# Spreading the output projection of a decode attention kernel over its rolled loop

## The chip, the cores and the metric

One core of one Trainium2 chip. The metric is device time in microseconds (us), the median of the fast runs; lower is better. The profile's "span" is some 1.8 us shorter than the time.

## The reference, cut to what matters

One decode step: 32 query heads share 8 groups of keys and values (4 heads to a group), 65536 keys of 128 elements, all in bf16. A small dense layer on another input (`B_*`) is added to the result.

```python
q = (x @ wq).reshape(B, Sq, 32, 128)            # x is one row of 512
k = jnp.repeat(k_cache, 4, axis=1)              # 8 groups, 65536 x 128 each
p = softmax(q @ k.T / sqrt(128)); o = p @ v     # 134 MB of keys, 134 MB of values
attention = o.reshape(1, 1, 4096) @ wo          # wo is 4096 x 512, 4 MB
# ... layer norm ahead of wq, GELU layer B, sum of both: 512 outputs
```

With one query row every key and every value is read once and used once. 280.5 MB pass through the core; that is the job.

## The kernel before: the parts that matter

Keys and values come in 32 "units" of 16384 keys (four to a group): each is a 4 MB key chunk and a 4 MB value chunk. There are four 4 MB buffers, two for keys and two for values. A loop pass ("pair") handles two key chunks and the value chunks of the two units before them; TensorE's program is folded into a real loop of 15 passes, the other engines' programs are straight. For a key chunk TensorE transposes 128 tiles, VectorE (DVE) and ScalarE (ACT) copy them to SBUF, then come 128 score matmuls; for a value chunk, 128 PV matmuls (probabilities by values). "PV 30" is the PV of value chunk 30.

```python
def pair(i):
    ua, ub = 2 * i, 2 * i + 1
    transposes(0, 0); stats_1(); transposes(0, 1); stats_2(ua - 1); load_q(ua)
    transposes(0, 2); scores(0, 0); transposes(0, 3)
    done_chunk("K", ua)                 # the buffer is free: the next chunk is issued
    scores(0, 1); v_block(ua - 2, 0); scores(0, 2); v_block(ua - 2, 1)
    scores(0, 3); v_block(ua - 2, 2); v_block(ua - 2, 3)
    done_chunk("V", ua - 2); keep_o(ua - 2)
    # ... the same for ub
```

Each unit has its own maximum, so the 4 units of a group must be weighed before their sum. The kernel before does it after the loop, for 7 groups at once ("early"), then for the last ("late"). `wo` is loaded whole, in 4 pieces of 1 MB, during the loop.

```python
L = NU - 1                              # the last unit, 31
weights_1(*early); stats_1(); weights_2(*early); stats_2(L)
weights_3(*early); merged(*early)
wo_part(*early)                         # 112 matmuls 128x128 by 128x1, 28 heads
weights_1(*late)
pv(L - 1, range(TPD)); keep_o(L - 1)    # PV of value chunk 30
weights_2(*late); weights_3(*late); merged(*late)
for i in range(len(LASTP)):             # value chunk 31 comes in 5 pieces: 64, 32, 16, 8, 8 tiles
    pv(L, range(cuts[i], cuts[i + 1]), f"last{i}")
    if i == 0: wo_part(*late)           # 16 matmuls
    if i == 1: ...                      # finT (the sum so far) to rows: 4 f32 matmuls
# oL = chunk 31's part; 16 matmuls with wo; cast; store
```

Of the kernel before, what the change touches and what calls it, by code (L numbers as in the profile page):

```python
# [5 lines left out]
BF = mybir.dt.bfloat16  # L6
# [37 lines left out]
class _Sched:  # L44
# [61 lines left out]
    def op(self, eng, fn, reads=(), writes=(), publish=True):  # L106
        req = self._required(reads, writes)
        waits = self._waits_for(eng, req)
        if publish:
            eng.count += 1  # L110
            snap = dict(eng.clock)
            snap[eng.sem] = eng.count
            ev = _Ev(eng.sem, eng.count, snap, eng)
            for dev in eng.deferred:
                dev.val = ev.val
                dev.snap = snap
            eng.deferred = []
            pub = (eng.sem, 1)
        else:
            ev = _Ev(eng.sem, None, None, eng)  # L120
            eng.deferred.append(ev)
            pub = None
        self._record(ev, reads, writes)
        eng.ops.append((waits, fn, pub))
        return ev
# [99 lines left out]
def bass_parallel_sum__gqa_block_cached__dense_activation_gelu__decode_kernel(  # L225
# [87 lines left out]
    wo_sb = nc.alloc_sbuf_tensor("wo_sb", [128, H, D], BF)  # L313
# [15 lines left out]
    oT_bf = nc.alloc_sbuf_tensor("oT_bf", [128, H], BF)  # L329
# [25 lines left out]

    for t, res in ((ident_bf, "ident_bf"), (ident_f, "ident_f")):
        sch.op(POOL, lambda t=t: pool.memset(t[:, :], 0.0), writes=[res])
        sch.op(
            POOL,
            lambda t=t: pool.affine_select(  # L360
                out=t[:, :], in_=t[:, :], compare_op=ALU.not_equal, fill=1.0,
                base=0, pattern=[[-1, 128]], channel_multiplier=1,
            ),
            reads=[res], writes=[res],
        )
# [61 lines left out]
    def dma_wo(q):  # L427
        hs = slice(q * H // 4, (q + 1) * H // 4)
        sch.dma(
            SP,  # L430
            lambda hs=hs: sp.dma_start(
                out=wo_sb[:, hs, :],
                in_=A_wo[hs.start * DH:hs.stop * DH, :].rearrange("(h p) n -> p h n", p=128)),
            sem_wo, writes=[f"wo{q}"], total=64)
# [3 lines left out]
    for q in range(4):  # L438
        after_chunk[("V", 6 + 4 * q)] = [lambda q=q: dma_wo(q)]
# [192 lines left out]

    def pair(i):
# [3 lines left out]
        def v_block(u, s):  # L637
            if not first:
                pv(u, range(s * TPB, (s + 1) * TPB))
# [13 lines left out]
        if first:  # L653
            layernorm()
            qproj()
            load_q(ua)
            scores(0, 0)
        scores(0, 1)
        v_block(ua - 2, 0)
        scores(0, 2)  # L660
        v_block(ua - 2, 1)
        scores(0, 3)
# [24 lines left out]
        if first:  # L687
            ffn2()
            issue_chunks()
        else:  # L690
            done_chunk("V", ub - 2)
            keep_o(ub - 2)

# [9 lines left out]
    negm_v = negm[:, :].rearrange("p (g h j) -> p g h j", h=CPG, j=HPG)  # L703
    coef_v = coef[:, :].rearrange("p (g h j) -> p g h j", h=CPG, j=HPG)
    nmin_v = nmin[:, :].rearrange("p (g j) -> p g j", j=HPG)
    rden_v = rden[:, :].rearrange("p (g j) -> p g j", j=HPG)
    osum_v = o_sum[:, :].rearrange("p (g j) -> p g j", j=HPG)
    wtot_r = wtot[:, :].rearrange("p (g h j) -> p g j h", h=CPG, j=HPG)
    oc_r = o_c[:, :].rearrange("p (g h j) -> p g j h", h=CPG, j=HPG)
    negm_r = negm[:, :].rearrange("p (g h j) -> p g j h", h=CPG, j=HPG)  # L710

    def part(n, g0, g1):
        return n, slice(g0, g1), slice(g0 * CPG * HPG, g1 * CPG * HPG), slice(g0 * HPG, g1 * HPG), \
            range(g0 * CPG, g1 * CPG)

    def weights_1(n, gs, cs, hs, us):
        neg = [f"negm{u}" for u in us]
        sch.op(DVE, lambda: dve.tensor_reduce(out=nmin_v[:, gs, :], in_=negm_r[:, gs], axis=AX.X, op=ALU.min),
               reads=neg, writes=[f"nmin{n}"])
        for h in range(CPG):  # L720
            sch.op(DVE, lambda h=h: dve.tensor_tensor(out=coef_v[:, gs, h, :], in0=nmin_v[:, gs, :],
                                                      in1=negm_v[:, gs, h, :], op=ALU.subtract),
                   reads=[f"nmin{n}"] + neg, writes=[f"coef{n}_{h}"])
        sch.op(ACT, lambda: act.activation(out=coef[:, cs], in_=coef[:, cs], func=ACTF.Exp),
               reads=[f"coef{n}_{h}" for h in range(CPG)], writes=[f"coef{n}"])

    def weights_2(n, gs, cs, hs, us):
        at = slice(PA_SUM + cs.start, PA_SUM + cs.stop)
        sch.op(PE, lambda: pe.matmul(pA[:, at], lhsT=ones_f[:, :], rhs=sums[:, cs], start=True, stop=True),  # L729
               reads=["ones_f"] + [f"sums{u}_{j}" for u in us for j in range(HPG)], writes=["pA"])  # L730

    def weights_3(n, gs, cs, hs, us):
        at = slice(PA_SUM + cs.start, PA_SUM + cs.stop)
        sch.op(DVE, lambda: dve.tensor_tensor(out=wtot[:, cs], in0=coef[:, cs], in1=pA[:, at], op=ALU.mult),
               reads=[f"coef{n}", "pA"], writes=[f"wtot{n}"])
        sch.op(DVE, lambda: dve.tensor_reduce(out=rden_v[:, gs, :], in_=wtot_r[:, gs], axis=AX.X, op=ALU.add),
               reads=[f"wtot{n}"], writes=[f"rden{n}"])
        sch.op(DVE, lambda: dve.reciprocal(out=rden[:, hs], in_=rden[:, hs]), reads=[f"rden{n}"],
               writes=[f"rden{n}"])
        for h in range(CPG):  # L740
            sch.op(DVE, lambda h=h: dve.tensor_tensor(out=coef_v[:, gs, h, :], in0=coef_v[:, gs, h, :],
                                                      in1=rden_v[:, gs, :], op=ALU.mult),
                   reads=[f"coef{n}", f"rden{n}"], writes=[f"coefr{n}_{h}"])

    def merged(n, gs, cs, hs, us):
        done = [u for u in us if u < L]
        ks = slice(cs.start, cs.start + len(done) * HPG)
        if len(done) < len(us):
            sch.op(DVE, lambda: dve.memset(o_c[:, ks.stop:cs.stop], 0.0), writes=[f"o_z{n}"])
        sch.op(DVE, lambda: dve.tensor_tensor(out=o_c[:, ks], in0=o_all[:, ks], in1=coef[:, ks], op=ALU.mult),  # L750
               reads=[f"coefr{n}_{h}" for h in range(CPG)] + [f"o{u}" for u in done], writes=[f"o_c{n}"])
        sch.op(DVE, lambda: dve.tensor_reduce(out=osum_v[:, gs, :], in_=oc_r[:, gs], axis=AX.X, op=ALU.add),
               reads=[f"o_c{n}"] + ([f"o_z{n}"] if len(done) < len(us) else []), writes=[f"o_sum{n}"])
        sch.op(DVE, lambda: dve.tensor_copy(out=oT_bf[:, hs], in_=o_sum[:, hs]), reads=[f"o_sum{n}"],  # L754
               writes=[f"oT{n}"])

    def wo_part(n, gs, cs, hs, us):
        heads = range(hs.start, hs.stop)
        for kt in range(KT):
            for h in heads:  # L760
                sch.op(
                    PE,
                    lambda kt=kt, h=h: pe.matmul(  # L763
                        pA[:, PA_AT + kt:PA_AT + kt + 1], lhsT=wo_sb[:, h, kt * 128:(kt + 1) * 128],
                        rhs=oT_bf[:, h:h + 1], start=h == hs.start, stop=h == hs.stop - 1),
                    reads=[f"wo{h * 4 // H}", f"oT{n}"], writes=["pA"],
                    publish=kt == KT - 1 and h == hs.stop - 1,
                )
        sch.op(DVE, lambda: dve.tensor_tensor(out=finT[:, :], in0=pA[:, PA_AT:PA_AT + KT], in1=finT[:, :],
                                              op=ALU.add), reads=["pA", "finT"], writes=["finT"])  # L770

    early, late = part("e", 0, G - 1), part("l", G - 1, G)
    weights_1(*early)
    stats_1()
    weights_2(*early)
    stats_2(L)
    weights_3(*early)
    merged(*early)
    wo_part(*early)
    weights_1(*late)  # L780
    pv(L - 1, range(TPD))
    keep_o(L - 1)
    weights_2(*late)
    weights_3(*late)
    merged(*late)
# [3 lines left out]
    for i in range(len(LASTP)):  # L789
        pv(L, range(cuts[i], cuts[i + 1]), f"last{i}")  # L790
        if i == 0:
            wo_part(*late)
        if i == 1:
            for kt in range(KT):
                sch.op(PE, lambda kt=kt: pe.matmul(pR[32 * kt:32 * kt + 1, 0:128], lhsT=finT[:, kt:kt + 1],
                                                   rhs=ident_f[:, :], start=True, stop=False),
                       reads=["finT", "ident_f"], writes=[f"pss{(L - 1) % 2}"],
                       publish=kt == KT - 1)
    sch.op(DVE, lambda: dve.tensor_tensor(out=oL_bf[:, :], in0=pO[:, 0:HPG], in1=coef[:, L * HPG:], op=ALU.mult),
           reads=["pO", "coefrl_3"], writes=["oL"])  # L800
    for j in range(HPG):
        for kt in range(KT):
            sch.op(PE, lambda j=j, kt=kt: pe.matmul(
                pR[32 * kt:32 * kt + 1, 0:128], lhsT=oL_bf[:, j:j + 1],
                rhs=wo_sb[:, H - HPG + j, kt * 128:(kt + 1) * 128], start=False, stop=j == HPG - 1),
                reads=["oL", "wo3"], writes=[f"pss{(L - 1) % 2}"],
# [63 lines left out]
```

## Time and profile before

| | before |
|---|---|
| time, median | 671.12 us (671.02 to 671.37) |
| span of the profiled run | 669.4 us |
| bytes read | 280.5 MB |
| busy: transfers (16 engines, data queue), TensorE, DVE, ACT | 98.2%, 83%, 39%, 36% |
| last PV matmul ends | 666.2 us |
| last piece of the last value chunk lands | 659.9 us |

The windowed view of the kernel before. Columns: window (us), its length, busy time and instructions of TensorE (PE), its weight loads (PEld), DVE, ACT, GpSimd (POOL), then TensorE's granted clock, the busy share of the transfer engines, and GB/s.

```profile
20.00:145.00 125.00, 108.34 (x2380) 102.18 (x2378) 52.09 (x113) 49.05 (x90) 0.00 (x0) 0.77 1.00 428
145.00:340.00 195.00, 164.68 (x3814) 155.78 (x3811) 77.89 (x153) 71.51 (x133) 0.00 (x0) 0.75 1.00 427
340.00:640.00 300.00, 254.55 (x5878) 240.76 (x5876) 121.49 (x235) 113.97 (x220) 0.00 (x0) 0.76 1.01 431
...
654.00:655.00 1.00, 1.00 (x44) 1.00 (x41) 0.00 (x0) 0.00 (x0) 0.00 (x0) 0.50 0.97 389
...
657.00:658.00 1.00, 0.58 (x22) 0.52 (x20) 0.00 (x0) 0.00 (x0) 0.00 (x0) 0.50 0.47 170
...
659.00:660.00 1.00, 0.37 (x14) 0.37 (x14) 0.00 (x0) 0.00 (x0) 0.00 (x0) 0.50 0.03 12
```

Read the last two columns. From 20 to 640 us the transfer engines never pause (share 1.00 to 1.01, 427 to 431 GB/s). They run out one after another between 655 and 660 us: some finish their share earlier than others. I take from it that nothing done inside the loop can help as long as this stream stays as it is (x_pe24 and x_dma below test it); what can be won lies behind the transfers.

The chain of waits of the kernel before, from 560 us on (start, us, what):

```profile
563.39 28.29 DMA kv<-in_A_k_cache_dram
591.73 3.60 PE pst L477 x32
...
603.17 27.41 DMA kv<-in_A_k_cache_dram
630.63 3.60 PE pst L477 x32
...
652.30 3.15 PE pA L763 x112
655.45 2.13 PE pO L552 x80
657.58 2.05 issue
659.63 1.42 PE pO L552 x48
```

In the loop the chain is "a key chunk lands, TensorE transposes it, the buffer is free, the next key chunk is issued and takes 27 us to land". At the end it leaves the transfers and follows TensorE. There TensorE's timeline is the thing to read (start, us, engine, line, operation, output<-inputs, shapes, count, and in brackets the idle time before it and what ended it):

```profile
649.11 0.58 PE L528 MATMUL pA<-diag,ones_f 4*128 4x4 f32 x2
652.30 3.15 PE L763 MATMUL pA<-oT_bf,wo_sb 128*128 128x1 bf16 x112 [2.60 <-DVE oT_bf L754]
655.31 2.27 PE L552 MATMUL pO<-P_bf,kv 128*128 128x4 bf16 x80
659.63 1.42 PE L552 MATMUL pO<-P_bf,kv 128*128 128x4 bf16 x48 [2.05 <-issue]
660.91 0.59 PE L729 MATMUL pA<-sums,ones_f 128*128 128x16 f32 x2
661.34 1.85 PE L552 MATMUL pO<-P_bf,kv 128*128 128x4 bf16 x64
...
665.15 1.01 PE L552 MATMUL pO<-P_bf,kv 128*128 128x4 bf16 x32
666.41 0.60 PE L803 MATMUL pss<-wo_sb,oL_bf 128*1 128x128 bf16 x16 [0.25 <-DVE oL_bf L799]
```

TensorE waits 2.60 us for DVE's weights of 28 heads, runs the 112 `wo` matmuls, and only then starts the PV of value chunk 30 (655.31), and in its middle stands still for 2.05 us with nothing to wait for. So it finishes 6.3 us after the last piece landed. Where that piece landed is read from the line that issues the five pieces of chunk 31 (first and last start of an issue; times from issue to landing):

```profile
L396 SPq DMA_DIRECT2D kv<-in_A_v_cache_dram x5: 328/422/435, 628.8 to 630.9; - x5
...
DMA to landing us min/median/max: 26.2/28.9/29.2
```

The two last pieces (256 KB each) have a median of 29.0 us in the list of transfers: 630.9 + 29.0 = 659.9 us.

### The profile page before, as it was taken

Reading aid. Unit: us, or ns where it says so; the run is one execution under the profiler, and the core shown is the slowest. Engines: PE = TensorE matmul, PEld = TensorE weight load, DVE = VectorE, ACT = ScalarE, POOL = GpSimd, SP = SyncE. Lnnn points to the kernel's source line nnn. Section 1 sums busy time; section 2 is a strip of 40 time slices with the busy share of each in tenths; the row PEclk is TensorE's granted clock in tenths of the full one; section 3 lists DMA queues with packets and bytes.
Section 4 is the critical chain, followed back from the end, with each engine's and each line's share of the span. In section 5 each row is a group of like instructions: output and inputs, shape, how many; then the busy total and the mean of one; then the engine's idle time right before and its main releaser. Section 6 shows DMA issues by size and latency. Waiting matters only on the chain.

```text
span 669.4 us, 27324 instructions
## 1 busy us (share of the span) xinstructions
PE 555.8 (83%) x12818; PEld 525.2 (78%) x12818; DVE 264.1 (39%) x548; ACT 243.5 (36%) x455; POOL 1.3 (0%) x10
## 2 busy tenths in 40 slices
PE   2799769999868889688888888698888889888887
PEld 2688669999857879587887778697877889778876
DVE  0445324444433344343344433244433344443451
ACT  1354224444422444332344323344422434432340
POOL 0000000000000000000000000000000000000000
PEclk9786678888867888676788667787766788766775
DMA  9999999999999999999999999999999999999992
GB/s 376 420 436 423 434 425 430 431 431 433 417 429 435 429 433 414 433 429 435 431 415 435 429 431 431 417 429 433 429 433 435 427 433 433 431 429 435 426 423 106
DMA packets 14708, 280.83 MB, mean 420 GB/s; under 512 B 1498, under 2 KB 5596, under 8 KB 5980
## 3 DMA queue, kind: packets, MB, share of 16 engines
q1 hardware_dynamic: 14684, 280.51, 98.2%
q8 instruction: 15, 0.25, 0.1%
q14 instruction: 9, 0.07, 0.0%
HBM read 280.50 MB, written 0.00 MB: 419 GB/s over the span
## 4 chain that ended last, share of the span: by engine, by line
DMA 56%; PE 39%; issue 2%; ACT 1%; DVE 1%
DMA kv<-in_A_k_cache_dram 56%; PE pst L477 27%; PE pss L497 5%; PE pO L552 3%; PE pA L518 1%; PE pA L528 1%; PE pA L763 1%; PE pA L570 1%; PE pA L585 1%; ACT kt_ring L487 0%; PE pA L612 0%; ACT P_bf L538 0%; ACT L538 0%; ACT L462 0%; PE pA L729 0%
## 5 line engine op out<-in xcount | busy, mean ns | idle before, releaser
L477 PE MATMUL pst<-ident_bf,kv 128*128 128x128 bf16 x4096 | 314.5, 246 | 90.4 <-DMA kv<-in_A_k_cache_dram 88.8
L477 PEld LDWEIGHTS pst<-ident_bf,kv 128*128 128x128 bf16 x4096 | 286.3, 112 | 109.7 <-DMA kv<-in_A_k_cache_dram 77.7
L487 ACT ACTIVATE kt_ring<-pst 128x1024 bf16<-128x1024 bf16 x192 | 197.8, 1031 | 396.4 <-PE pst L477 393.7
L485 DVE COPY kt_ring<-pst 128x1024 bf16<-128x1024 bf16 x320 | 211.6, 688 | 221.8 <-PE pst L477 221.2
L552 PE MATMUL pO<-P_bf,kv 128*128 128x4 bf16 x4096 | 120.4, 165 | 11.7 <-issue 11.7
L552 PEld LDWEIGHTS pO<-P_bf,kv 128*128 128x128 bf16 x4096 | 113.8, 100 | 12.6 <-issue 12.6
L497 PE MATMUL pss<-q_cur,kt_ring 128*128 128x4 bf16 x4096 | 121.2, 164 | 1.9 <-issue 1.4
L497 PEld LDWEIGHTS pss<-q_cur,kt_ring 128*128 128x128 bf16 x4096 | 114.7, 97 | 2.1 <-issue 1.5
L505 DVE TENSOR_REDUCE pmax<-pss 128x4 f32<-128x512 f32 x32 | 22.1, 692 | 117.9 <-PE pss L497 117.9
L538 ACT ACTIVATE P_bf<-pss,negm 128x128 bf16<-128x128 f32 x128 | 50.8, 551 | 1.4 <-DVE negm L531 1.4
L538 ACT ACTIVATION_READ_ACCUMULATOR P_bf<-pss,negm 128x1 f32 x128 | 36.1, 282 | 0.0
L561 DVE COPY o_all<-pO 128x4 f32<-128x4 f32 x31 | 5.0, 162 | 42.1 <-PE pO L552 42.1
L518 PE MATMUL pA<-ident_f,pmax 128*4 128x128 f32 x64 | 17.0, 363 | 0.0
L528 PE MATMUL pA<-diag,ones_f 4*128 4x4 f32 x64 | 12.4, 261 | 0.0
L528 PEld LDWEIGHTS pA<-diag,ones_f 4*128 4x128 f32 x64 | 9.6, 186 | 3.4 <-issue 0.2
L520 DVE TENSOR_REDUCE gmax<-pA 4x1 f32<-4x128 f32 x32 | 8.6, 268 | 0.0
L522 DVE TENSOR_SCALAR diag<-ident_f,gmax 4x4 f32<-4x4 f32 x32 | 7.0, 217 | 1.1
L518 PEld LDWEIGHTS pA<-ident_f,pmax 128*4 128x4 f32 x64 | 2.9, 84 | 5.4 <-DVE kt_ring L485 4.5
L763 PE MATMUL pA<-oT_bf,wo_sb 128*128 128x1 bf16 x128 | 3.7, 165 | 2.7 <-DVE oT_bf L754 2.6
L763 PEld LDWEIGHTS pA<-oT_bf,wo_sb 128*128 128x128 bf16 x128 | 3.6, 104 | 2.8 <-DVE oT_bf L754 2.7
L531 DVE TENSOR_SCALAR negm<-pA 128x4 f32<-128x4 f32 x32 | 5.1, 160 | 1.1 <-PE pA L528 1.1
L570 PE MATMUL pA<-xnT_bf,kv 128*128 128x1 bf16 x128 | 3.5, 164 | 1.8 <-DVE xnT_bf L465 1.8
(63 smaller groups left out, 38.3 us busy)
## 6 DMA issues: line engine op xcount, KB each, us to landing
kv<-in_A_k_cache_dram SPq DMA_DIRECT2D x32, 4096.0 KB, 27.9
kv<-in_A_v_cache_dram SPq DMA_DIRECT2D x31, 4096.0 KB, 31.8
kv<-in_A_wq_dram SPq DMA_DIRECT2D x1, 4096.0 KB, 20.0
wo_sb<-in_A_wo_dram SPq DMA_DIRECT2D x4, 1024.0 KB, 34.2
kv<-in_B_w_dram SPq DMA_DIRECT2D x2, 1792.0 KB, 36.5
kv<-in_A_v_cache_dram SPq DMA_DIRECT2D x1, 2048.0 KB, 26.2
kv<-in_A_v_cache_dram SPq DMA_DIRECT2D x1, 1024.0 KB, 28.3
kv<-in_A_v_cache_dram SPq DMA_DIRECT2D x1, 512.0 KB, 29.1
```

The lines of the kernel that those rows point to most:

```text
L477: lambda tb=tb, at=at, b=b, tt=s * TPB + t: pe.transpose(pst[tb][:, at * 128:(at + 1) * 128], slot[b][:, tt, :], ident_bf[:, :]),
L485: e, fn = DVE, lambda tb=tb, dst=dst: dve.tensor_copy(out=dst, in_=pst[tb][:, :])
L487: e, fn = ACT, lambda tb=tb, dst=dst: act.activation(out=dst, in_=pst[tb][:, :], func=ACTF.Copy)
L497: lambda k=k, kb=kb, at=at, t=t: pe.matmul(pss[k][:, at:at + HPG], lhsT=kt_ring[:, kb * BCOL + t * 128:kb * BCOL + (t + 1) * 128], rhs=q_c ...
L505: lambda k=k: dve.tensor_reduce(out=pmax[:, :], in_=pss[k][:, 0:CW].rearrange("p (t j) -> p j t", j=HPG), axis=AX.X, op=ALU.max),
L518: sch.op(PE, lambda: pe.matmul(pA[0:HPG, PA_ST:PA_ST + 128], lhsT=pmax[:, 0:HPG], rhs=ident_f[:, :], start=True, stop=True), reads=["pmax" ...
L520: sch.op(DVE, lambda: dve.tensor_reduce(out=gmax4[:, :], in_=pA[0:HPG, PA_ST:PA_ST + 128], axis=AX.X, op=ALU.max), reads=["pA"], writes=[" ...
L528: sch.op(PE, lambda: pe.matmul(pA[:, PA_SB:PA_SB + HPG], lhsT=ones_f[0:HPG, 0:128], rhs=diag4[0:HPG, 0:HPG], start=True, stop=True), reads ...
L538: lambda k=k, u=u, j=j, src=src: act.activation(out=P_v[k][:, :, j], in_=src[:, :, j], func=ACTF.Exp, bias=negm[:, u * HPG + j:u * HPG + j ...
L552: lambda k=k, b=b, t=t: pe.matmul(pO[:, 0:HPG], lhsT=slot[b][:, t, :], rhs=P_v[k][:, t, :], start=t == 0, stop=t == TPD - 1),
L570: lambda h=h, kt=kt: pe.matmul(pA[:, PA_Q + h:PA_Q + h + 1], lhsT=wq_sb[:, kt, h * DH:(h + 1) * DH], rhs=xnT_bf[:, kt:kt + 1], start=kt == ...
L763: lambda kt=kt, h=h: pe.matmul(pA[:, PA_AT + kt:PA_AT + kt + 1], lhsT=wo_sb[:, h, kt * 128:(kt + 1) * 128], rhs=oT_bf[:, h:h + 1], start=h ...
```

## The change

The intent: take the 28 heads' weights and their 112 `wo` matmuls out of the tail. In each pass, beside the loop's own work, DVE weighs one group every second pass, TensorE adds one 128x128 by 128x16 matmul for the totals and 8 `wo` matmuls (two heads), and the `wo` rows of those heads come as a piece of 256 KB. As TensorE's program is one loop body, passes without a group do dummy work that keeps the semaphore counts equal (`inc=3`, `inc=7`).

```diff
-    wo_sb = nc.alloc_sbuf_tensor("wo_sb", [128, H, D], BF)
+    wo_cur = nc.alloc_sbuf_tensor("wo_cur", [128, HW, D], BF)        # HW = 2 heads
+    wo_end = nc.alloc_sbuf_tensor("wo_end", [128, HT, D], BF)        # the last 6 heads
 ...
+    def dma_wo_cur(k):
+        sch.dma(SP, lambda: sp.dma_start(out=wo_cur[:, :, :],
+            in_=A_wo[k * HW * DH:(k + 1) * HW * DH, :].rearrange("(h p) n -> p h n", p=128)),
+            sem_misc, writes=["wo_cur"])
 ... in pair(i), g, odd = divmod(i - 3, 2):
         scores(0, 1)
+            if g >= 0 and not odd:  weigh_1(g)          # minimum, differences, sums; exp on ACT
+            else:                   ...                 # dummies, inc=3
         v_block(ua - 2, 0)
+            total()                                     # ones x sums_cur on TensorE
         scores(0, 2)
         v_block(ua - 2, 1)
+            if g >= 0 and not odd:  weigh_2(g); weigh_3(g, CPG); heads(...oT_cur); heads(...oT_next)
+            else:                   ...                 # oT_cur <- oT_next, inc=7
 ... at the end of the pass:
+            wo_part(wo_cur, "wo_cur", oT_cur, "oT_cur", HW)
+            if 2 <= i < NU // 2 - 1:  dma_wo_cur(i - 2)
 ... after the loop:
-    weights_1(*early); stats_1(); weights_2(*early); stats_2(L)
-    weights_3(*early); merged(*early); wo_part(*early); weights_1(*late)
+    stats_1()
+    wo_part(wo_end, "wo_end", oT_next, "oT_next", HW)
+    stats_2(L)
+    weigh_1(GL)
     pv(L - 1, range(TPD)); keep_o(L - 1)
+    total(); weigh_2(GL); ...; weigh_3(GL, CPG - 1); heads(GL, 0, HPG, oT_bf, "oT")
```

## The prediction

> **What bounds it now.** The transfers. In the windowed view the DMA engines are busy 1.00 at 427 to 433 GB/s from 3 to 640 us of a 669.4 us span; the bytes (280.5 MB) stay the same. TensorE has slack in the loop: from 145 us on, the chain of waits alternates some 11 us of work with 27 to 31 us of waiting for a key chunk. DVE is 39% busy, ACT 36%.
>
> Only the end is bound otherwise. DMA throughput falls from 389 GB/s at 655 us to 12 at 659.5 us, yet the last PV matmul ends at 666.2 us, and 3.2 us of fixed work follow (oL, 16 matmuls, cast, store). The timeline shows why: value chunk 30 (I estimate it landed near 650.2 us, 19.5 us of streaming after key chunk 31) is not touched until 655.3 us, because TensorE waits 2.6 us for the weights of 28 heads on DVE (to 652.3 us), then runs 112 wo matmuls (3.1 us). Inside PV comes a 2.05 us "issue" gap (657.58 to 659.63 us).
>
> I read that gap as instruction fetch. [...] between the issue gaps after 68 and 72 us lie 126 matmuls of two instructions plus 4 register adds, 256 in all. Under full DMA load a block arrived 5.5 to 7 us after the previous one was entered.
>
> **What the change does.**
> - Loop: 8 wo matmuls (0.2 us at 27 ns spacing), one f32 ones-matmul (0.5 us), some seven DVE operations of 0.16 to 0.35 us per pass, all inside the waits for key chunks: worth 0. The loop grows to near 1605 instructions[...].
> - Transfers: 13 pieces of 256 KB plus one of 768 KB for four of 1 MB; same 1 KB rows, behind 27 us of backlog: 0, perhaps +0.5 us. In the first 145 us TensorE paces, but the least backlog I work out is 2.9 MB (6.7 us): no starving.
> - Tail: 112 wo matmuls become 8; the 28-head weights leave DVE. PV of chunk 30 then starts on landing, near 650.3 us instead of 655.3, and ends near 654, before the first piece of the last chunk lands (655.0).
> - The fetch gap moves, it does not go. By instruction counts the block boundary lies near the 51st matmul of PV 30 (651.7 us), the next near the 49th of the last chunk's PV; its block arrives near 658. Then 15 PV, 16 wo, 32 PV, finT matmuls and 32 PV end near 661.3, the span near 664.5.
>
> **Prediction.** About 4.8 us saved, of the 6 us between now and the last landing plus fixed work (663.2): 671.12 falls to **666.3 us**, range 664.6 to 668.8. Faster by over 2%: 0.01; within 2%: 0.97; slower by over 2%: 0.02.
>
> **What would show it.** GB/s in the middle unchanged; DMA still running out near 659 to 660 us; PV 30 starting at 650 to 651 us; an "issue" gap of 1 to 2 us inside the last chunk's first 64 PV matmuls; the end 3.2 us after the last PV.
>
> **What would make it wrong.** No fetch gap (then about 665). A loop no longer resident, with issue gaps in every pass. Small wo transfers slowing the stream by microseconds. The last weights on DVE holding back wo and finT.

The sum comes to 666.3 us: the last PV at 661.3 us in place of 666.2, 3.2 us of fixed work behind it, and the 1.8 us by which the time exceeds the span; loop and transfers 0. That the grown loop would run without fetching its instructions again was my estimate at that point; p_pad57 and p_pad84 below test it.

## The result and the profile after

| | before | after |
|---|---|---|
| time, median | 671.12 us | 666.37 us (666.03 to 666.68) |
| span of the profiled run | 669.4 us | 664.6 us |
| value chunk 30: PV starts | 655.31 us | 650.92 us |
| "issue" gap in the tail | 2.05 us | 0.39 us |
| last piece lands | 659.9 us | 660.8 us |
| last PV matmul ends | 666.2 us | 661.3 us |

The ratio is 0.9929 (95% interval 0.9911 to 0.9946). Such a ratio is the mean time of one kernel's fast runs over that of the other's of the same rounds, so it is not quite the ratio of the medians quoted.

The windowed view after, with the same columns:

```profile
20.00:145.00 125.00, 108.66 (x2476) 103.17 (x2474) 54.11 (x123) 50.73 (x94) 0.00 (x0) 0.78 1.00 427
...
340.00:640.00 300.00, 255.23 (x5889) 242.09 (x5885) 126.69 (x287) 112.10 (x218) 0.00 (x0) 0.76 1.01 429
...
657.00:658.00 1.00, 0.61 (x23) 0.53 (x21) 0.00 (x0) 0.00 (x0) 0.00 (x0) 0.50 0.45 174
...
659.00:660.00 1.00, 1.00 (x32) 0.64 (x28) 0.00 (x0) 0.00 (x0) 0.00 (x0) 0.50 0.07 25
```

In its middle the stream is what it was. In the 300 us from 340 us on DVE has 287 instructions in place of 235, and the GB/s differ by 2. TensorE's timeline of the tail:

```profile
649.50 0.58 PE L538 MATMUL pA<-diag,ones_f 4*128 4x4 f32 x2 [0.25 <-DVE finT L700]
650.92 3.57 PE L562 MATMUL pO<-P_bf,kv 128*128 128x4 bf16 x128 [0.83 <-DMA kv<-in_A_v_cache_dram]
654.35 0.59 PE L665 MATMUL pA<-sums_cur,ones_f 128*128 128x16 f32 x2
655.95 1.36 PE L562 MATMUL pO<-P_bf,kv 128*128 128x4 bf16 x46 [1.01 <-DVE o_c L680]
657.70 0.64 PE L562 MATMUL pO<-P_bf,kv 128*128 128x4 bf16 x18 [0.39 <-issue]
658.20 0.57 PE L695 MATMUL pA<-oT_bf,wo_end 128*128 128x1 bf16 x16
658.62 0.99 PE L562 MATMUL pO<-P_bf,kv 128*128 128x4 bf16 x32
...
660.09 1.20 PE L562 MATMUL pO<-P_bf,kv 128*128 128x4 bf16 x32
661.54 0.59 PE L825 MATMUL pss<-wo_end,oL_bf 128*1 128x128 bf16 x16 [0.25 <-DVE oL_bf L821]
```

Now PV of chunk 30 waits for its data (the bracket names the transfer) and runs through in one go. The wait before chunk 31 is put down to DVE's `o_c`, but those matmuls do not read it; their first piece (2048 KB) was issued at 627.9 us and took 27.9 us, so it landed at 655.8 us, and that is the wait. The pieces of chunk 31 after the change:

```profile
L405 SPq DMA_DIRECT2D kv<-in_A_v_cache_dram x5: 328/432/433, 627.9 to 629.7; - x5
...
DMA to landing us min/median/max: 27.9/30.8/31.2
```

629.7 + 31.1 (the median of the two last pieces) = 660.8 us. TensorE is now only half a microsecond behind the transfers.

### The profile page after: what moved, and what is told of

Same layout as the page of the kernel before. It is cut to its first block, busy times and chain, and to the rows that moved or that the text cites. A ratio compares the mean times of both kernels' runs of the same rounds, so it can differ in the third digit from the quotient of the medians.

```text
span 664.6 us, 27512 instructions
## 1 busy us (share of the span) xinstructions
PE 556.8 (84%) x12862; PEld 527.2 (79%) x12862; DVE 273.7 (41%) x628; ACT 244.5 (37%) x469; POOL 2.3 (0%) x13
## 4 chain that ended last, share of the span: by engine, by line
DMA 58%; PE 38%; issue 2%; ACT 1%; DVE 0%
DMA kv<-in_A_k_cache_dram 54%; PE pst L487 26%; PE pss L507 4%; DMA kv<-in_A_v_cache_dram 4%; PE pO L562 3%; PE pA L528 1%; PE pA L538 1%; PE pA L580 1%; PE pA L595 1%; ACT kt_ring L497 0%; PE pA L622 0%; ACT P_bf L548 0%; ACT L548 0%; ACT L472 0%; PE pA L665 0%
## 5 line engine op out<-in xcount | busy, mean ns | idle before, releaser
L562 PEld LDWEIGHTS pO<-P_bf,kv 128*128 128x128 bf16 x4096 | 114.2, 101 | 13.1 <-issue 11.0
L507 PEld LDWEIGHTS pss<-q_cur,kt_ring 128*128 128x128 bf16 x4096 | 116.3, 98 | 1.8 <-issue 1.2
L665 PE MATMUL pA<-sums_cur,ones_f 128*128 128x16 f32 x32 | 6.4, 277 | 0.0
L695 PE MATMUL pA<-oT_cur,wo_cur 128*128 128x1 bf16 x120 | 5.3, 166 | 0.0
L665 PEld LDWEIGHTS pA<-sums_cur,ones_f 128*128 128x128 f32 x32 | 5.2, 205 | 0.0
## 6 DMA issues: line engine op xcount, KB each, us to landing
kv<-in_A_v_cache_dram SPq DMA_DIRECT2D x1, 2048.0 KB, 27.9
```

Of the source, the lines that this page charges most:

```text
L507: lambda k=k, kb=kb, at=at, t=t: pe.matmul(pss[k][:, at:at + HPG], lhsT=kt_ring[:, kb * BCOL + t * 128:kb * BCOL + (t + 1) * 128], rhs=q_c ...
L562: lambda k=k, b=b, t=t: pe.matmul(pO[:, 0:HPG], lhsT=slot[b][:, t, :], rhs=P_v[k][:, t, :], start=t == 0, stop=t == TPD - 1),
L665: sch.op(PE, lambda: pe.matmul(pA[:, PA_SUM:PA_SUM + GW], lhsT=ones_f[:, :], rhs=sums_cur[:, :], start=True, stop=True), reads=["ones_f", ...
```

## The experiments

Theory: the gain is one of position. PV of chunk 30 starts when its data is there, because nothing stands before it any more; the work put into the loop is free, because the stream of bytes sets the pace; and what is left of the distance to the transfers depends on where TensorE's program crosses from one block of 256 instructions to the next. The blocks are read from the kernel before's trace: its six "issue" gaps between 30 and 100 us lie 768, 512, 256, 512 and 256 of TensorE's instructions apart (matmuls, weight loads and register operations). Each ends 1.3 to 1.6 us after the end of a packet of 16 KB on the instruction queue q8, and 5.6 to 7.0 us after the 256 instructions before it began. The 128 matmuls of PV 30 with their weight loads are 256 instructions and took 3.57 us in the changed kernel, less than those 5.6 to 7.0 us. Where TensorE took longer over 256 instructions (75.94 to 84.09 us), a packet ended within them (80.73 us) and no gap followed. Rivals: the gap is a wait for data; less work in total; pieces of 256 KB help or hurt the stream. The second falls by the counts of the two profiles: the work did not shrink (12862 matmuls in place of 12818, 628 DVE instructions in place of 548).

### b_swap: only the order in the tail

The kernel before, with nothing spread.

```diff
-    wo_part(*early)
-    weights_1(*late)
     pv(L - 1, range(TPD))
     keep_o(L - 1)
+    wo_part(*early)
+    weights_1(*late)
```

> Kernel before with one thing moved: the PV matmuls of value chunk 30 ahead of the 112 wo matmuls in the tail; nothing spread over the loop. Theory (position plus instruction fetch): PV 30 starts on landing (near 651 us), the 112 wo matmuls then run after it, and the fetch gap moves into them (near the 65th, about 1.5 to 2 us, to 658 us); the last PV ends near 664.7 us, span near 667.9 us, time near 669.6 us: about a third of the gain. Rival (the gain is only the 5 us by which PV 30 started late, fetch plays no part): span near 665.5 us, time near 667.2 us.

Measured: 669.31 us, ratio to before 0.9976 (0.9961 to 0.9991). The timeline:

```profile
649.84 3.57 PE L552 MATMUL pO<-P_bf,kv 128*128 128x4 bf16 x128 [0.42 <-DMA kv<-in_A_v_cache_dram]
653.28 1.84 PE L763 MATMUL pA<-oT_bf,wo_sb 128*128 128x1 bf16 x64
657.14 1.42 PE L763 MATMUL pA<-oT_bf,wo_sb 128*128 128x1 bf16 x48 [2.02 <-issue]
```

PV of chunk 30 starts 5.5 us earlier, and yet only 1.8 us are won (the rival's 667.2 us is out): the `wo` matmuls now stand in the way of chunk 31, and the gap sits after the 64th of them, where the count of instructions put it (65th). Removing the lateness of one step is not enough; the 3.2 us of `wo` work and the gap have to go as well.

### c_weights: the weights in the loop, the matmuls in the tail

The changed kernel, with `wo` loaded as before and its 28 heads' matmuls in the tail.

```diff
-            wo_part(wo_cur, "wo_cur", oT_cur, "oT_cur", HW)          # in each pass
-            if 2 <= i < NU // 2 - 1:  dma_wo_cur(i - 2)
+    for q in range(4): after_chunk[("V", 6 + 4 * q)] = [lambda q=q: dma_wo(q)]   # 4 x 1 MB
 ... after the loop
     stats_1()
-    wo_part(wo_end, "wo_end", oT_next, "oT_next", HW)
+    wo_part(wo_sb, "wo0", oT_all, "oT_all", H - HPG)
```

> Changed kernel with the wo matmuls of 28 heads put back into the tail, and wo loaded in four pieces of 1 MB; the group weights stay beside the loop. Theory (position plus instruction fetch): the 112 wo matmuls fill the idle time before value chunk 30 lands, so they cost only about 1.5 us of delay of PV 30 (to 652.5 us), but the tail is 104 matmuls longer, so a block boundary falls into PV 30 with a gap of 1 to 2 us; last PV near 662.8 us, time near 667.9 us, 1.5 us above the changed kernel. Rival (no fetch): the last PV as in the changed kernel, 661.3 us, time 666.4 us.

Measured: 668.11 us, ratio to before 0.9958 (0.9943 to 0.9974); the last PV matmul ends at about 662.6 us.

```profile
649.17 3.15 PE L691 MATMUL pA<-oT_all,wo_sb 128*128 128x1 bf16 x112 [0.37 <-DVE gmax L526]
...
653.09 2.32 PE L558 MATMUL pO<-P_bf,kv 128*128 128x4 bf16 x81
656.31 1.41 PE L558 MATMUL pO<-P_bf,kv 128*128 128x4 bf16 x47 [0.90 <-issue]
```

Taken in this order, about 3.0 of the 4.8 us come from the weights and 1.7 us from the matmuls. Most of the 112 matmuls hide in the time in which chunk 30 has not landed, as expected; the rest shows as a later PV (653.09 us) and a gap (0.90 us, a little under the 1 to 2 expected). This kernel loads `wo` in 1 MB pieces, and its last piece lands at 660.8 us, as in the changed kernel with its thirteen pieces of 256 KB. Smaller pieces cost nothing here, behind a stream that was busy throughout (DMA share 1.00 to 1.01 from 20 to 640 us).

### b_pad20 and p_pad57: is the gap an instruction fetch?

Idle matmuls before the first key chunk lands, when TensorE has nothing to do (in the kernel before it waits for that chunk until 13.1 us). They are to move every later block boundary by their number; nothing else is edited.

```diff
+    for t in range(PAD):     # 20 in the kernel before, 57 in the changed one
+        sch.op(PE, lambda: pe.matmul(pO[:, 64:68], lhsT=ident_bf[:, :], rhs=ident_bf[:, 0:4],
+               start=True, stop=True), reads=["ident_bf"], writes=["pO"], publish=t == PAD - 1)
```

> Kernel before with 20 idle matmuls before the first key chunk lands. If the 2.05 us gap inside PV 30 (after its 81st matmul) is the fetch of a block of 256 instructions, it moves to after the 61st matmul, begins about 0.5 us earlier, and ends about 0.5 us earlier; the gaps in the first loop pass move by 20 matmuls too. If it is a wait for data, it stays after the 81st. Time unchanged within 0.6 us.

Measured: one run, 671.92 us (0.8 us over the median of before, a little more than expected; its whole tail began 0.84 us later, PV 30 at 656.15 us). The gap moved from after the 80th or 81st matmul (two records of the trace differ by one) to after the 61st:

```profile
656.15 1.77 PE L552 MATMUL pO<-P_bf,kv 128*128 128x4 bf16 x61
659.77 1.95 PE L552 MATMUL pO<-P_bf,kv 128*128 128x4 bf16 x67 [1.85 <-issue]
```

Twenty idle matmuls 640 us earlier moved it by twenty matmuls. A wait for data should have stayed. But it ended at 659.77 us and not some 0.5 us earlier than before, as I had expected. In three runs of the kernel before (before, b_pad20 and b_dve80, below) PV 30 starts at 655.31, 656.15 and 657.10 us, and the gap ends at 659.63, 659.77 and 659.63 us: its end does not follow TensorE. It follows the packet that brings the block: in all ten runs with one "issue" gap in the tail (p_pad84 apart) the gap ends 1.2 to 1.5 us after the end of the first packet of the tail on TensorE's instruction queue, q8 (here 658.25, 658.34 and 658.40 us, by the packets in the kept traces). Why that packet comes so late is not shown.

> Changed kernel with 57 idle matmuls (114 instructions) before the first key chunk lands, nothing else, so that every later block boundary comes 57 matmuls earlier. Theory: the gap after the 46th matmul of the last chunk's PV is gone, because that boundary now falls near matmul 118 of PV 30[...]; the next one falls near the finT matmuls. Last PV near 660.7 us, time 0.3 to 0.9 us below the changed kernel (near 665.8 us). Rival (the gap is a wait for data or for DVE): the gap stays after about the 46th matmul, time unchanged.

Measured: 666.26 us, ratio to before 0.9928 (0.9915 to 0.9942): the changed kernel's time. The gap is gone, and the time is not better:

```profile
655.87 1.85 PE L562 MATMUL pO<-P_bf,kv 128*128 128x4 bf16 x64 [0.99 <-DVE o_c L680]
...
659.80 0.80 PE L562 MATMUL pO<-P_bf,kv 128*128 128x4 bf16 x24
660.83 0.38 PE L562 MATMUL pO<-P_bf,kv 128*128 128x4 bf16 x8 [0.24 <-DMA kv<-in_A_v_cache_dram]
```

The first 64 matmuls run through, and the last 8 wait for the last piece. The time I expected to win was below what the transfers allow: the last piece lands at 660.7 us, not at the 659.9 us that I had read from the kernel before. The changed kernel is at that limit, whether or not it has its gap; the 0.3 to 0.9 us expected from its removal are not there.

### x_pe24 and x_dma: what is free and what is not

x_pe24 adds 24 `wo` matmuls of no use to every pass (and 104 idle ones ahead, so that the tail's boundaries keep their place).

```diff
             wo_part(wo_cur, "wo_cur", oT_cur, "oT_cur", HW)
+            for t in range(24):
+                sch.op(PE, ... pe.matmul(pA[:, PA_AT + 4:PA_AT + 5], lhsT=wo_cur[...], rhs=oT_cur[...]) ...)
```

> Changed kernel with 24 more wo matmuls in every loop pass (four times the 8 that the change added; their results are not used), and 104 idle matmuls before the first key chunk so that the block boundaries of the tail stay where they are. Theory (work added to the loop falls into the waits for key chunks): unchanged, 666.4 us within 0.6. Rival (TensorE's added work is on the path): 15 passes of about 0.9 us, 13 us more, near 680 us.

Measured: 666.5 us, ratio to before 0.9929 (0.9913 to 0.9946). With the 8 of the change these are 32 in each pass, four times what the change added, and they cost nothing.

x_dma loads each 256 KB piece a second time, into a buffer of its own that nothing reads.

```diff
+        sch.dma(SP, lambda: sp.dma_start(out=wo_dup[:, k * HW:(k + 1) * HW, :],
+            in_=A_wo[k * HW * DH:(k + 1) * HW * DH, :]...), sem_dup, writes=[f"wo_dup{k}"], total=13 * 16)
```

> Changed kernel that loads each of its 13 pieces of wo a second time into a buffer that nothing reads: 3.41 MB more. Theory (the stream of bytes sets the time, and the change is free in it only because its bytes are the same): 3.41 MB at 429 GB/s, 7.9 us more, near 674.3 us. Rival (the queue has slack that small pieces use): under 1 us more.

Measured: 676.1 us, ratio to before 1.0076 (1.0059 to 1.0092). Against the changed kernel (666.4 us) that is 9.7 us for 3.41 MB, so 351 GB/s for these rows of 1 KB, where the stream as a whole runs at 429. The theory holds, its size was off by 1.8 us: `wo` costs about a fifth more per byte than the caches do. The packets in the kept traces say that it is the rows: a packet of 1 KB took 46 ns (356 GB/s on 16 engines), one of 32 KB, as the caches come, 1216 ns (431 GB/s). Both kernels load `wo` in rows of 1 KB (median packet 48 ns before, 46 ns after), so both pay for it.

### p_pad84: when the loop no longer fits

As p_pad57, with 84 idle matmuls. The loop has as many instructions, but by my count begins and ends so that it touches eight blocks of 256 and not seven.

> Changed kernel with 84 idle matmuls (168 instructions) before the first key chunk, so that the loop, still about 1605 instructions, starts 168 instructions later and touches eight blocks of 256 in place of seven. [...] every pass fetches its blocks again: over 100 fetches of 16 KB on the instruction queue in place of 14, issue gaps of 1 to 6 us in every pass, 700 to 800 us. Rival[...]: 15 fetches, unchanged near 666.3 us.

Measured: 735.17 us (734.1 to 737.66), ratio to before 1.0968 (1.0944 to 1.0992). The queue of TensorE's instructions:

```profile
q8 instruction: 78, 1.28, 0.7%
```

(before: 15 packets; after: 14. In both, 12 of them come between 23 and 103 us and the others after 655 us: over the later passes, of 1605 to 1611 instructions each after the change, none was fetched.) q14 stayed at 10 packets, so q8 is taken for TensorE's. And the longest waits of TensorE in that run (line, waited for, us in total, times, longest):

```profile
PE pst L487 <- issue: 84.5, 15, 7.6
PE pO L562 <- issue: 48.5, 17, 4.0
PE pss L507 <- issue: 10.7, 9, 2.5
PE pst L487 <- DMA kv<-in_A_k_cache_dram: 8.4, 1, 8.4
```

By the times of those packets, every second pass fetches nine blocks again (I expected every pass). TensorE is no longer waiting for keys: the chain of waits is 77% TensorE and 20% issue. Between "nothing" and 69 us lie 54 instructions of padding. By my count in the changed kernel itself the loop ends about 120 instructions before the end of its seventh block (the gap in the last chunk, counted back, gives it), an estimate that the two runs bracket: with 114 instructions of padding q8 carried 15 packets (p_pad57), with 168 it carried 78. By this estimate some 60 further matmuls in the loop would do the same.

### b_dve80, x_dve390, after_again: why the last piece lands later

The last landing had moved from 659.9 to 660.8 us, and that is what now bounds the kernel. It was at 659.7 to 659.9 us in before, b_pad20 and b_swap, and at 660.7 to 660.8 us in the changed kernel, p_pad57 and c_weights. These three have the weights beside the loop, which means about 80 more DVE instructions, and one packet more on the queue that carries the other engines' instructions (q14: 10 in place of 9, of 8 KB each).

```diff
 b_dve80 (kernel before):
+    for t in range(80):      # ahead of the first pair
+        sch.op(DVE, lambda t=t: dve.memset(spare[:, t % 2:t % 2 + 1], 0.0), writes=[f"spare{t % 2}"])
 x_dve390 (changed kernel), at the end of each pass:
+            for t in range(26):
+                sch.op(DVE, lambda t=t: dve.memset(spare[:, 0:1], 0.0), writes=["spare0"])
```

> Kernel before with 80 tiny memsets on DVE at its start (as many DVE instructions as the change adds). The last piece of the last value chunk landed at 659.8 to 659.9 us in the kernel before, in its padded form and with PV 30 moved, but at 660.8 to 660.9 us in the three kernels with the group weights beside the loop, whichever way wo was loaded. If the longer DVE program (one more 8 KB fetch in the stream) delays it, the last piece lands near 660.8 us here too. If it is the loop's work on TensorE, ACT or DVE that does it, the last piece lands near 659.9 us as before. The time itself should not move by more than 0.6 us.

Measured: one run, 671.21 us; the time is unchanged, as the kernel before does not end with the transfers. (Its tail began 1.8 us later, but the "issue" gap shrank to 0.26 us and ended at 659.63 us as before.) The pieces of chunk 31:

```profile
L396 SPq DMA_DIRECT2D kv<-in_A_v_cache_dram x5: 327/422/435, 629.1 to 631.2; - x5
...
DMA to landing us min/median/max: 26.8/29.5/29.7
```

631.2 + 29.6 = 660.8 us, with 10 packets on q14. Eighty DVE instructions run at the start of the kernel made the last transfer land 0.9 us later at its end.

> Changed kernel with 26 tiny memsets on DVE at the end of each of the 15 loop passes (390 instructions, about 3 more 8 KB fetches in the stream[...]). If each such fetch delays the slowest transfer engine by about 0.9 us, as the step from 9 to 10 suggested, the last piece lands near 663.5 us and the time rises by about 2.5 us, to 668.9. If the step had another cause, the last piece lands near 660.8 us and the time stays at 666.4.

(For the queue q14, 13 packets in place of 10 were expected.)

Measured: 669.35 us, ratio to before 0.9975 (0.9958 to 0.9992), so 2.95 us over the changed kernel in the same rounds; 13 packets on q14. The last piece lands at 631.7 + 32.1 = 663.8 us, and TensorE waits for it:

```profile
q14 instruction: 13, 0.11, 0.0%
```

```profile
663.87 0.38 PE L562 MATMUL pO<-P_bf,kv 128*128 128x4 bf16 x8 [0.28 <-DMA kv<-in_A_v_cache_dram]
```

(In this kernel the last 26 memsets also fall into the tail and delay PV 30 to 655.0 us; the bracket shows that the end was nevertheless set by the data.) Three more packets, 2.7 to 3.0 us later.

The kept traces also show the way in which a fetch does this. They hold the start, length, size and queue of every packet, and each 4 MB chunk ends on each of the 16 transfer engines with a packet of 4 bytes, so there are 16 end times for each chunk. How far each lies behind the first of the 16 (the lag of that engine) stays the same from chunk to chunk within 0.2 us, except after an instruction packet, when one lag grows. The lags that grew at DVE's packets (told from the others by the count of DVE operations between them: 127 and 125 in the kernel before) join up into the lag of one engine:

| | DVE's packets in the stream (us from the span's start) | lag of that engine, us |
|---|---|---|
| before | 220.8, 384.5, 547.7 | 1.5, 2.4, 3.4, 4.4 |
| x_dve390 | 153.3, 228.7, 307.8, 386.6, 469.3, 549.6, 628.6 | 1.3, 2.3, 3.2, 4.2, 5.2, 6.2, 7.2, 8.1 |

So all of DVE's packets after 100 us put the same transfer engine back, by 0.97 us each, though a packet itself took 0.32 us. (ACT's do it to another engine, by 0.7 us each.) The other engines lag by at most 3.7 us, so DVE's engine is the last from its third such packet on in the kernel before (547.7 us); from there every fetch moves the last landing. In x_dve390 it moves its last data at 663.4 us, when all others have been done since 658.9 us. Why a packet costs three times its own length is not shown.

> Changed kernel once more, on the same chip, for the place of the last landing and of the gap: last piece near 660.8 us, gap of 0.3 to 1.0 us after the 46th matmul of the last chunk, 666.4 us.

Measured: 666.4 us, ratio to before 0.993 (0.9913 to 0.9947); last piece at 661.1 us; gap 0.22 us.

### v_pool: an attempt at a better version

The changed kernel with 57 idle matmuls and with the SBUF-only part of the weights on GpSimd, DVE down from 629 to 573 instructions (628 to 571 in the profiles).

```diff
-        sch.op(DVE, lambda: dve.tensor_tensor(out=o_c[:, ks], in0=o_all[:, ks], in1=coef[:, ks], op=ALU.mult), ...)
-        sch.op(DVE, lambda: dve.tensor_reduce(out=o_sum[:, hs], in_=oc_r[:, g, :, 0:n], ...), ...)
+        sch.op(POOL, lambda: pool.tensor_tensor(out=o_c[:, ks], ...), ...)
+        for h in range(1, CPG):  sch.op(POOL, ... pool.tensor_tensor(out=o_sum, ..., op=ALU.add), ...)
 # likewise the differences, the totals and their reciprocal; the minimum, the PSUM read and a copy stay on DVE
```

> Attempt at a better version: the changed kernel with the 57 idle matmuls, and with the SBUF-only part of the group weights in the loop (and nine small operations of the first pair) moved from DVE to the idle GpSimd, so that DVE has 573 instructions in place of 629 and stays under the count at which its next 8 KB block is fetched before the end. If that fetch is what delays the last landing by 0.9 us,[...] the last piece lands near 660.0 us, and the time is 0.7 to 1.0 us below the changed kernel's, near 665.5 us. If not, it is the changed kernel's 666.4 us.

(9 packets in place of 10 were expected on q14.)

Measured: 666.4 us, ratio to before 0.993 (0.9917 to 0.9944): no gain. q14 carried 11 packets: by their times DVE's fifth block was still fetched (at 639.0 us), and GpSimd's longer program brought one of its own (at 308.2 us). The last piece landed at 660.9 us, so GpSimd's packet did not add to the delay: it put another engine back, from a lag of 0.05 to 0.72 us. The count at which DVE's fifth block is fetched was my estimate, and wrong. (A first build of this kernel deadlocked in the simulator, because I had dropped the ACT dummy that keeps the counts of the passes equal.)

> Changed kernel a third time, on the same chip and in the same rounds as v_pool, to compare with: 666.4 us, ratio to before 0.993.

Measured in the same rounds: 666.19 us, ratio to before 0.9928 (0.9914 to 0.9941); last piece at 660.7 us. No version beat the changed kernel clearly.

## Why the prediction was right, point by point

The predicted time was 666.3 us and the measured one 666.37 us. Part of that precision is luck. The prediction let the last PV matmul end at 661.3 us because a block arrives near 658 us and some 3.3 us of work follow. It did end at 661.3 us, but the block came 0.3 us earlier (657.7 us), so that the work behind it could have ended about 661.1 us; the last 8 matmuls then waited some 0.2 us (the last 32 took 1.20 us, and 1.01 in the kernel before) for a piece that landed 0.9 us later than in the kernel before (660.8 us). p_pad57, which has no gap and the same time, shows that the landing is what binds.

- **The transfers bound the kernel, the loop's work is free.** Right. GB/s from 340 to 640 us are 429 after and 431 before; x_pe24 shows that 360 more matmuls cost nothing, x_dma that 3.41 MB more cost 9.7 us.
- **PV of chunk 30 starts on landing, at 650 to 651 us.** Right: 650.92 us, waiting for its transfer. It ends at 654.4 us (predicted near 654).
- **The gap moves into the last chunk's PV.** Right in place (after the 46th matmul; predicted near the 49th), and shown to be an instruction boundary by b_pad20, whose gap moved by the twenty matmuls that were added. **Its size was wrong**: 0.39 us, and 0.20 to 0.22 us in the repeats (1.02 us in x_pe24), in place of 1 to 2 us. The matmuls before it started late, because the first piece of chunk 31 landed at 655.8 us and not at 655.0, and the block arrived at 657.7 us and not at 658.
- **"DMA still running out near 659 to 660 us".** Off by 0.9 us: 660.8 us. The term "Transfers: 0, perhaps +0.5" looked at the pieces of `wo`, which c_weights shows to be neutral. What moved the landing was outside the sum, DVE's longer program: one more packet on q14 (10 in place of 9), and 0.97 us on one transfer engine for each of DVE's. b_dve80 isolates it, x_dve390 triples it, and the packets show the one engine on which it falls.
- **Fixed work of 3.2 us after the last PV.** It is 3.3 us: the span ends at 664.6 us.
- **"No fetch gap (then about 665)".** Wrong: p_pad57 has no gap and takes 666.26 us, because the last landing is the next limit.

Of the 4.8 us, c_weights puts about 3.0 on the weights that left the tail and 1.7 on the matmuls. That a fetch of DVE's instructions holds up one particular transfer engine is shown by the packets of the kept traces. It is also a part of why the engines end at different times (655 to 661 us): besides DVE's and ACT's packets, TensorE's of the first pass leave engines behind (in before one lag grew from 2.1 to 3.6 us after the packet at 101.7 us). That the fetches explain the whole spread was not worked out, and why DVE's always fall on the same engine stays open.

## What to carry to other kernels

When the transfers are busy from start to end, look only at what happens after them: which of the last chunks waits for something that could have been done earlier, and in which order the engine meets that work. Work that moved from the tail into a loop with slack was free here as long as TensorE's loop was not fetched again: with 114 instructions of padding ahead of it (seven blocks by my count) q8 carried 15 packets and the time was 666.26 us; with 168 (eight blocks), and as many instructions in the loop, 78 packets and 735.17 us. It also lengthened DVE's straight program: one more packet on q14, and each of DVE's put back by 0.97 us the transfer engine that was the last to finish. Before expecting the next microsecond, find the next limit: removing the gap here was worth nothing, since the last landing was already there.
